# Softmax reciprocal as the exponential of a negative logarithm on ScalarE, and a third pairwise add on VectorE in the fourth block

## The chip, the cores and the metric

The kernel runs on one core of a Trainium2 chip. The metric is the device time of one execution in microseconds (us). The kernel before takes 184.47 us, the median of 4 runs that lie between 183.99 and 184.72. One further execution was recorded by the hardware profiler; all durations below are from that execution.

## The reference

The reference normalizes the input over its 512 features, and adds two branches to the input: a local attention with 32 heads of 16 features, and a gated feed-forward network.

```python
def _A_ref(x, wqkv, wo):
    B, S, D = x.shape              # 1, 2048, 512
    H = 32; Dh = D // H            # 16
    W, dil = 8, 2
    q, k, v = ...                  # x @ wqkv, split into 32 heads
    idx = pos[:, None] - off[None, :]      # off = 0, 2, ..., 14
    kg, vg = ...                   # keys and values at the 8 positions
    logits = jnp.einsum("bhsd,bhswd->bhsw", q, kg) * Dh ** -0.5
    logits = jnp.where(mask, logits, -1e9)
    attn = _softmax(logits, axis=-1)       # over 8 positions
    o = jnp.einsum("bhsw,bhswd->bhsd", attn, vg)
    return o.reshape(B, S, D) @ wo

def _B_ref(x, w_gate, w_up, w_down):       # 512 -> 1376 -> 512
    h = _gelu(x @ w_gate) * (x @ w_up)
    return h @ w_down

xn = _layernorm(x, axis=-1)
return x + _A_ref(xn, A_wqkv, A_wo) + _B_ref(xn, B_w_gate, B_w_up, B_w_down)
```

Each token attends to only eight positions, at distances 0, 2, ..., 14. So the logits are no matrix product over tokens; they are elementwise products of queries with shifted keys, summed over the 16 features of a head.

## The kernel before

**Blocks.** The 2048 tokens are cut into 4 blocks of 512. Feature data lies with features on the 128 partitions and the block's tokens along the free dimension, in four groups of 128 features. Each block passes through the same steps, and steps of neighbouring blocks are interleaved.

**Steps of block b**, with the names of the code. The input is normalized (`bnst`, `bnag`, `sub`, `norm`; on ScalarE also small steps `ve`, `vp`, `va`, `vb`) and transposed by DMA (`trx`, from block 1 on). TensorE computes the q, k and v projections (`mm<b>_<0,1,2>_<g>`, L1009, four matmuls each), and ScalarE copies them out of PSUM (`evq`, `evk`, `evv`, L1020). VectorE multiplies queries with the eight shifted keys (`pr<b>_<g>`, L1040, 128x4096), once for each of the four groups, and adds the products in pairs: `pa<b>_0` adds groups 0 and 1, `pa<b>_1` adds groups 2 and 3 (L1053). TensorE then sums over the features of a head with a matrix of constants, in `er<b>_3`. This task first computes a small part of the feed-forward network (L1078, 16 matmuls), and then, for each of the two half sums, 8 matmuls of 32x512 (L1085) that accumulate the logits in two PSUM banks.

**Softmax.** VectorE takes the maximum over the eight positions (`d1`, L1117) and subtracts it (`d2`, L1122). ScalarE takes the exponential (`exp`, L1131). VectorE adds the eight exponentials in three steps (`d4a`, `d4b`, `d4c`, L1138), takes the reciprocal of the 128x128 sums (`d5`, L1150) and multiplies (`d6`, L1155). Four DMAs write the result to a scratch tensor in DRAM (`ss`, L1164), and four read it back, spread over the features of each head, into PT (`sl`, L1176). VectorE multiplies it with the shifted values (`pv`, L1184), adds (`pw`, L1193, `pz`, L1199), and the attention's output stands in OT.

**Feed-forward and output.** TensorE computes the gate and up projections (`fg`, `fu`, L1217, four matmuls each, and `fg<b>_10`, L1256); ScalarE applies gelu (`gelu`, L1227, L1264) and copies the up half (`uev`, L1234, L1272); VectorE multiplies (`h`, L1241, L1279). The output tile of 128 tokens sums 4 matmuls with Wo and 11 with Wd (`acc...`, L1302). ScalarE copies it (`fe`, L1335), VectorE adds the input (`fin`, L1340, L1346), and a DMA stores it (`sto`).

**What sets the order.** The order of every engine's instructions is written out by hand in a table `ORDER`, one list of task names for each of TensorE ("pe"), ScalarE ("act"), VectorE ("dve"), GpSimd ("pool") and SyncE ("sp"), which issues all DMAs. An engine works through its list strictly in order; waits on other engines follow from the data and from the buffers. PSUM has eight banks, taken in the order in which tasks ask for them, so a TensorE task may also wait until another engine has read an older result out of a bank. `schedule` (L207) walks the lists to choose buffers and banks; `emit_engine` (L364) emits them. ScalarE holds one set of function tables at a time; where the next function is not in the set, the build puts a table load ahead of it. Identity and Square need no change of set here.

Of the kernel before, what the change touches and what calls it, by code (L numbers as in the profile page):

```python
# [135 lines left out]
class Graph:  # L136
# [252 lines left out]
    def report(self):  # L389
# [8 lines left out]
ACTF = mybir.ActivationFunctionType  # L398
# [6 lines left out]
    "pe":  # L405
        "warm0 warm1 warm2 warm3 warm4 warm5 warm6 warm7 warm8 warm9 tpx0_0 warm10 warm11 warm12 warm13 "
        "warm14 mma0_0 tpx0_1 mmt0_0 mmt0_1 mmt1_0 tpx1_0 mmt1_1 mmt0_2 tpx1_1 mmt1_2 mmt0_3 mmt1_3 "
        "mm0_2_0_0 mm0_2_3_0 mm0_2_2_0 mm0_2_1_0 fg0_0 fg0_1 fg0_2 fu0_0 fg0_3 fu0_1 fu0_2 fg0_4 fu0_3 fg0_5 "
        "fu0_4 fu0_5 fg0_6 fg0_7 er0_3 mm1_0_0_0 mm1_1_0_0 mm1_0_1_0 mm1_1_1_0 fg1_0 fu0_6 mm1_0_3_0 "
        "mm1_0_2_0 mm1_1_3_0 fu0_7 fu1_0 fg1_1 fg0_8 fu1_1 mm1_1_2_0 fu0_8 mm1_2_0_0 fg1_2 fg0_9 fu1_2 "  # L410
        "mm1_2_2_0 fg1_3 fu1_3 fu0_9 fg0_10 fg1_4 fu1_4 mm1_2_3_0 fg1_5 mm1_2_1_0 fg1_6 fu1_5 fu1_6 fg1_7 "
        "mm2_0_0_0 mm2_1_1_0 mm2_1_0_0 mm2_0_3_0 er1_3 mm2_0_1_0 fg1_10 mm2_1_2_0 mm2_2_1_0 mm2_0_2_0 fu1_7 "
        "fg2_0 accd1 mm2_1_3_0 accd2 fg2_1 mm2_2_3_0 mm2_2_2_0 fg1_8 fg2_2 acca0 fu2_0 accb0 fg1_9 mm2_2_0_0 "
        "accd3 er2_3 fu2_1 fu1_8 fu1_9 fu2_2 fg2_3 fu2_3 mm3_1_2_0 mm3_1_1_0 mm3_1_3_0 mm3_0_1_0 mm3_0_0_0 "
        "fg2_4 mm3_1_0_0 fu2_4 mm3_0_2_0 fg3_0 mm3_0_3_0 fu3_0 fg3_1 fg2_10 fg3_2 accd7 accd5 mm3_2_0_0 "
        "fg2_5 fu3_1 fg3_3 mm3_2_3_0 mm3_2_1_0 fu2_5 fu3_2 acca4 er3_3 accb4 fg3_4 accd6 fu3_3 fu3_4 fg2_6 "
        "fg3_5 fu2_6 fg2_7 fg3_6 fu2_7 fg2_8 fu2_8 fu3_5 fg3_7 fu3_6 mm3_2_2_0 fg2_9 fu3_7 fu2_9 fg3_8 fu3_8 "
        "fg3_9 fg3_10 acca8 accd10 accd9 fu3_9 accb8 accd11 acca12 accd13 accd14_0 accd14_1 accw14_0 "
        "accw14_1 accw13 accb12 accd15_0 accw12 accw15_0 accd15_1 accw15_1 accd15_2 accw15_2",
    "act":  # L420
        "c_tbl sx1 sq0 negm1 sxx1 sq1 evx0_0 evx0_1 evq0_0 sq2 evq0_1 evk0_0 evx1_0 sq3 evk0_1 bnst8 evx1_1 "
        "bnst9 evq0_2 sq6 evk0_2 evq0_3 evk0_3 ve8 evv0_0_0 sq4 vp8 bnag8 bnag9 va8 gelu0_0 evv0_2_0 "
        "evv0_3_0 bnst10 gelu0_1 bnst11 uev0_2 gelu0_3 vb8 gelu0_4 uev0_1 uev0_3 ve10 gelu0_5 uev0_4 uev0_0 "
        "uev0_5 gelu0_2 halo1 vp10 gelu0_7 bnag10 bnag11 evq1_0_0 evk1_0_0 evv0_1_0 evq1_1_0 evk1_1_0 "
        "gelu0_6 exp0 sub11 evq1_3_0 evk1_3_0 evq1_2_0 va10 uev0_7 uev1_0 uev0_10c uev0_6 sub9 vb10 sub8 "
        "uev1_1 evk1_2_0 norm9 uev0_10b gelu1_1 gelu1_0 norm8 gelu0_8 evv1_0_0 gelu1_2 sub10 uev0_8 bnst12 "
        "gelu0_9 norm11 uev1_2 uev0_9 norm10 evv1_2_0 gelu1_4 gelu1_3 uev1_3 evv1_1_0 uev1_4 uev1_5 uev0_10a "
        "bnst13 gelu1_5 gelu0_10 uev1_6 evk2_1_0 evv1_3_0 evk2_0_0 ve12 vp12 gelu1_7 bnag12 evq2_0_0 gelu1_6 "
        "evq2_1_0 uev1_10b bnag13 uev1_10c halv1 evk2_2_0 evq2_2_0 halo2 exp1 bnst14 sub12 bnst15 uev1_7 "
        "va12 ve14 vb12 uev1_10a vp14 bnag14 evk2_3_0 bnag15 evq2_3_0 evv2_1_0 va14 vb14 fe1 fe2 sub14 "  # L430
        "gelu2_0 evv2_2_0 halo3 gelu1_10 sub15 uev2_0 norm12 sub13 evv2_0_0 evv2_3_0 norm13 fe0 norm15 fe3 "
        "norm14 gelu1_8 gelu2_1 gelu1_9 uev2_1 uev1_8 uev2_2 uev1_9 uev2_3 gelu2_2 evk3_2_0 evk3_1_0 "
        "uev2_10b gelu2_3 exp2 evq3_1_0 evk3_3_0 evq3_2_0 evq3_0_0 halv2 evk3_0_0 uev2_10c evq3_3_0 uev2_4 "
        "uev2_10a gelu2_10 gelu3_1 uev3_0 gelu3_0 fe7 evv3_0_0 gelu2_5 gelu3_3 evv3_1_0 uev2_5 uev3_1 fe5 "
        "gelu2_4 gelu3_2 uev3_10c halv3 evv3_3_0 uev3_2 fe4 fe6 uev3_3 uev3_10b exp3 gelu3_5 uev2_6 gelu3_4 "
        "gelu2_7 uev2_7 uev2_8 gelu3_6 gelu2_6 evv3_2_0 gelu3_7 uev3_4 gelu2_8 gelu2_9 uev2_9 uev3_10a "
        "uev3_7 uev3_5 uev3_6 gelu3_10 fe10 gelu3_8 gelu3_9 uev3_9 fe9 uev3_8 fe8 fe11 fe13 fe12",
    "dve":
        "c_wdz bnst0 bnag0 sub0 rstd0 norm0 mean1 sub1 evy0_0 rstd1 norm1 evy0_1 bnst2 bnag2 sub2 rstd2 "
        "norm2 bnst3 bnag3 sub3 rstd3 norm3 bnst7 bnst6 bnst5 bnag6 bnag7 bnst4 bnag5 sub7 rstd6 bnag4 sub6 "  # L440
        "norm7 sub4 sub5 norm6 pr0_2 pr0_0 pr0_3 rstd4 pr0_1 norm4 norm5 pa0_1 pa0_0 h0_0 h0_1 h0_2 mask "
        "d1_0 d2_0 pr1_0 pr1_1 d4a_0 d4b_0 d4c_0 d5_0 rstd8 d6_0 pr1_3 pa1_0 pr1_2 h0_3 pa1_1 pv0_1 rstd10 "
        "pv0_3 h0_4 pv0_0 h1_1 pv0_2 pw0_1 h0_10 pw0_2 d1_1 pw0_3 d2_1 pz0 pr2_2 d4a_1 pr2_0 d4b_1 h1_3 "
        "d4c_1 h1_2 d5_1 h1_0 d6_1 pr2_1 pr2_3 pa2_0 fin1 rstd12 pa2_1 h1_10 pv1_1 rstd14 pv1_3 d1_2 pv1_0 "
        "d2_2 pv1_2 pw1_1 fin3 pw1_2 h2_1 pw1_3 h1_4 d4a_2 pz1 d4b_2 pr3_1 d4c_2 pr3_2 d5_2 fin0 d6_2 pr3_3 "
        "pr3_0 h2_0 h2_10 pa3_0 fin2 pa3_1 pv2_0 pv2_2 d1_3 pv2_1 d2_3 pw2_1 h3_1 d4a_3 h3_0 d4b_3 fin7 "
        "d4c_3 h2_2 d5_3 fin5 d6_3 pv2_3 pw2_2 h2_3 pw2_3 h2_4 pz2 fin4 pv3_3 pv3_0 pv3_1 fin6 pw3_1 fin10 "
        "h3_3 h3_10 pv3_2 h3_2 fin9 h3_4 pw3_2 fin8 pw3_3 fin11 pz3 fin14_0 fin14_1 fin13 fin15_0 fin15_1 "
        "fin12 fin15_2",
    "pool":  # L450
        "c_ones c_onef c_id c_vnpad c_idb c_eps c_mhalf c_e8a c_e8b c_e8c c_e8d c_ktpad c_mask0 c_mask1 "
        "c_utz sq8 sq10 sq12 sq14",
    "sp":
        "ld_x0_0 ld_x0_1 ld_wq ld_x1_0 ld_wk ld_x1_1 ld_wv ld_x2 ld_x4 ld_x3 ld_wg0 ld_wu0 ld_wt0 ld_x5 "
        "ld_wt1 trx3_0 ld_wt2 trx3_1 trx2_0 trx2_1 ld_wd0 ld_x6 ldxr1 ld_x7 ld_wd1 ld_wo ss0_2 ss0_3 ss0_0 "
        "ss0_1 ldxr2 sl0_1 sl0_3 sl0_2 trx4_0 sl0_0 trx4_1 trx5_1 trx5_0 ss1_2 ss1_3 ss1_1 ss1_0 sl1_1 sl1_3 "
        "sl1_0 sl1_2 ldxr3 trx6_0 trx6_1 trx7_1 trx7_0 sto3 sto1 ldxr0 ldxr7 ss2_1 ss2_2 ss2_3 ss2_0 sl2_0 "
        "sl2_3 sl2_2 sto0 sl2_1 sto2 ldxr5 ldxr4 sto5 ss3_0 ss3_1 ss3_2 ss3_3 ldxr10 sl3_3 sl3_0 sl3_2 sl3_1 "
        "ldxr6 sto4 sto6 ldxr8 ldxr9 sto9 ldxr11 ldxr14 sto8 sto7 sto10 ldxr13 sto11 sto14_0 sto14_1 ldxr15 "
        "ldxr12 sto13 sto15_0 sto15_1 sto12 sto15_2",  # L460
}
SCHED = dict(DMA_BPUS=290e3, DMA_FIXED=1.7)
# [6 lines left out]
def d_act(n):  # L469
    return 0.10 + 0.00085 * n  # L470
# [10 lines left out]
def bass_parallel_sum__sliding_local_dilated__glu_gated_geglu__prompt_kernel(nc, A_x, A_wqkv, A_wo, B_x, B_w_gate, B_w_up, B_w_down, out, dbg=None, cfg=None):  # L481
    cfg = dict(cfg or {})
# [26 lines left out]
    PACT = cfg.get("PACT", 4)  # L509
    PPOW = cfg.get("PPOW", 4)  # L510
    FIN2 = cfg.get("FIN2", tuple(range(14)))
    PR_ADD3 = cfg.get("PR_ADD3", ())
    WO_LAST = cfg.get("WO_LAST", (3,))
    CHAIN_SHIFT = cfg.get("CHAIN_SHIFT", [0, 300, 600, 900])
    FFN_BASE = cfg.get("FFN_BASE", 500)
# [8 lines left out]
    with contextlib.ExitStack() as es:  # L524
        block = es.enter_context(nc.Block())

        def sb(name, shape, dt):
# [14 lines left out]
        mask = sb("mask", [32, 2, 4, 16], F32)  # L542
# [7 lines left out]
        sums = sb("sums", [128, 3], F32)  # L550
# [6 lines left out]
        rc = sb("rc", [128, NMS, 128], FP16)  # L557
# [3 lines left out]
        EX = sb("EX", [128, 1024], FP16)  # L561
# [23 lines left out]
        G = Graph()  # L585
# [81 lines left out]
            rd=[I_mask], wr=[I_mask], prio=PC2 + 10)  # L667
# [275 lines left out]
        for b in range(NB):  # L943
# [156 lines left out]
            def lgv(p0, np_, dims, lg=it_lg):  # L1100
                return bass.AP(PS, p0 * 4096 + 512 * lg.slot, [[4096, np_]] + [[st, n] for (st, n) in dims])

            def msv(k, it=it_ms):
                return bass.AP(ms, (it.slot * 2 + k) * 128, [[NMS * 2 * 128, 128], [1, 128]])
# [23 lines left out]
            it_ex = Item("ex%d" % b, P_ex, "ex")  # L1128

            def mk_d3(lgv=lgv):  # L1130
                return lambda e: e.activation(out=EX[:, :], in_=lgv(0, 128, [(1, 1024)]), func=ACTF.Exp)  # L1131
            G.task("act", "exp%d" % b, d_act(1024), mk_d3(), rd=[it_lg], wr=[it_ex], prio=base + 32,
                   table="exp", batch=b)

            for k, w in enumerate((512, 256, 128)):
                def mk_d4(w=w, it=it_pb, msv=msv):
                    def f(e):
# [6 lines left out]
                       rd=[it_ex if w == 512 else I_su], wr=[(it_ms, 1) if w == 128 else I_su],  # L1144
                       prio=base + 33)

            def mk_d5(msv=msv, it=it_ms):
                def f(e):
                    with nc.allow_low_precision(reason="the reference holds the sums of exponentials in bf16"):
                        return e.reciprocal(out=rc[:, it.slot, :], in_=msv(1))  # L1150
# [266 lines left out]
```

## Time and profile before

| | |
|---|---|
| median of 4 runs | 184.47 us (183.99 to 184.72) |
| profiled execution: time / span | 184.45 us / 182.6 us |
| TensorE matmuls busy | 178.0 us, 98% of the span |
| VectorE busy | 169.7 us, 93% |
| ScalarE busy | 128.2 us, 70% |
| GpSimd busy | 9.5 us, 5% |
| mean rate of the DMAs | 107 GB/s |
| granted TensorE clock | 1.000 |

The span runs from the first to the last instruction of the core; the rest of the execution's time lies around it. In the profile's rows PE is TensorE's matmul stream, PEld its weight loads, DVE is VectorE, ACT is ScalarE, POOL is GpSimd and SP is SyncE; L and a number is a line of the kernel. A row of a group shows the line, the engine, the operation, what is written and read with its shape, the count, the busy time and the mean duration in ns, and after the second bar the idle time ahead of it. A row of the chain or of a timeline shows a start in us, a duration in us and what ran. Neighbouring instructions of one engine overlap a little, so the step from one start to the next is shorter than the duration.

### The profile page before, as it was taken

The page shows a single profiled execution, that of the slowest core. Times are in us where ns is not written, and L with a number is a line of the kernel's source. Part 1 is how long each engine was busy: PE and PEld are TensorE (multiplying, and loading weights), DVE is VectorE, ACT ScalarE, POOL GpSimd, SP SyncE. Part 2 cuts the span into 40 slices and gives each one's busy share as a digit, 9 for nine tenths or more (in the row PEclk, how much of TensorE's full clock was granted, in tenths as well). Part 3 has the DMA queues.
Part 4 walks back from the last instruction along what each step waited for, and adds up shares of the span by engine and source line. Part 5 has one row for each costly group of instructions (what it writes and reads, how often), then busy time and mean ns, then how long its engine had stood idle before and what let it go on. Part 6 is the DMA issues. An engine that isn't in the chain of part 4 may idle for free.

```text
span 182.6 us, 2790 instructions
## 1 busy us (share of the span) xinstructions
PE 178.0 (98%) x1068; PEld 90.1 (49%) x1068; DVE 169.7 (93%) x172; ACT 128.2 (70%) x258; POOL 9.5 (5%) x23
## 2 busy tenths in 40 slices
PE   8799999999999999999999999999999999999994
PEld 2796444544444544444444544444444444444664
DVE  3769999999999999999999999999999999999922
ACT  5688987999999899998695977527449764234011
POOL 6000010003200000122000000000000000000000
DMA  5999915932672000002851020128100355022433
GB/s 137 354 378 379 122 24 137 364 105 52 178 147 57 0 0 0 4 14 77 249 67 30 9 77 0 31 58 263 53 0 0 92 149 196 0 86 61 140 103 102
DMA packets 26220, 19.60 MB, mean 107 GB/s; under 512 B 13824, under 2 KB 23008, under 8 KB 26208
## 3 DMA queue, kind: packets, MB, share of 16 engines
q1 hardware_dynamic: 26208, 19.44, 37.9%
q8 instruction: 8, 0.13, 0.3%
q14 instruction: 4, 0.03, 0.1%
HBM read 14.71 MB, written 3.15 MB: 98 GB/s over the span
## 4 chain that ended last, share of the span: by engine, by line
PE 94%; DMA 2%; ACT 1%; SPq 0%; issue 0%; DVE 0%; DVEq 0%
PE PS L1217 38%; PE PS L1302 29%; PE PS L1009 19%; PE PS L959 4%; DMA Wqkv<-in_A_wqkv_dram 2%; PE PS L1085 2%; PE PS L1256 2%; PE PS L1078 1%; SPq L731 0%; ACT KT L986 0%; ACT xnT L919 0%; PE PS L899 0%; DVE OB L1346 0%; DVEq L376 0%
## 5 line engine op out<-in xcount | busy, mean ns | idle before, releaser
L1302 PE MATMUL PS<-Wd,HT 128*128 128x512 bf16 (+2 forms) x209 | 41.0, 345 | 0.0
L1217 PE MATMUL PS<-xnT,Wg 128*128 128x512 bf16 x160 | 39.8, 379 | 0.0
L1217 PE MATMUL PS<-xnT,Wu 128*128 128x512 bf16 x160 | 39.1, 379 | 0.0
L1009 PE MATMUL PS<-xnT,Wqkv 128*128 128x512 bf16 x160 | 38.0, 379 | 0.0
L1184 DVE TENSOR_TENSOR UNI<-VN,PT 128x4096 f16<-128x4096 bf16 x16 | 36.3, 2282 | 0.0
L1040 DVE TENSOR_TENSOR UNI<-QT,KT 128x4096 f16<-128x4096 bf16 x16 | 36.1, 2283 | 0.0
L1302 PEld LDWEIGHTS PS<-Wd,HT 128*128 128x128 bf16 x209 | 19.6, 98 | 19.2 <-issue 0.4
L1234 ACT ACTIVATE UU<-PS 128x512 bf16<-128x512 f32 x40 | 23.1, 600 | 6.4 <-PE PS L1217 6.1
L1193 DVE TENSOR_TENSOR UNI<-UNI 128x4096 f16<-128x4096 f16 x12 | 27.4, 2285 | 0.0
L1227 ACT ACTIVATE GG<-PS 128x512 bf16<-128x512 f32 x40 | 22.9, 602 | 5.8 <-DVE HT L1241 5.8
L1009 PEld LDWEIGHTS PS<-xnT,Wqkv 128*128 128x128 bf16 x160 | 17.9, 113 | 16.9 <-issue 0.8
L1217 PEld LDWEIGHTS PS<-xnT,Wu 128*128 128x128 bf16 x160 | 15.6, 98 | 19.0 <-ACT XIN L853 0.4
L1217 PEld LDWEIGHTS PS<-xnT,Wg 128*128 128x128 bf16 x160 | 15.7, 98 | 18.7
L1335 ACT ACTIVATE OB<-PS 128x512 bf16<-128x512 f32 x14 | 8.3, 601 | 17.3 <-PE PS L1302 15.1
L1053 DVE TENSOR_TENSOR UNI<-UNI 128x4096 f16<-128x4096 f16 x8 | 18.2, 2282 | 0.0
L1302 PE MATMUL PS<-Wo,OT 128*128 128x512 bf16 (+2 forms) x76 | 16.5, 345 | 0.0
L1020 ACT ACTIVATE VN<-PS 128x512 bf16<-128x512 f32 x16 | 9.3, 596 | 6.5 <-PE PS L1009 6.5
L1241 DVE TENSOR_TENSOR HT<-GG,UU 128x1024 bf16<-128x1024 bf16 x20 | 13.5, 682 | 0.0
L832 POOL TENSOR_TENSOR sq<-ve,mhalf 128x2 bf16<-128x2 f32 x4 | 6.6, 1658 | 72.7 <-ACT ve L828 72.7
L1302 PEld LDWEIGHTS PS<-Wo,OT 128*128 128x128 bf16 x76 | 7.1, 98 | 6.6 <-issue 0.3
L1272 ACT ACTIVATE UT<-PS 64x256 bf16<-64x256 f32 (+1 forms) x12 | 5.4, 447 | 6.7 <-PE PS L1256 3.9
L959 PE MATMUL PS<-xnT,Wqkv 128*128 128x128 bf16 x128 | 8.1, 219 | 0.8 <-DMA Wqkv<-in_A_wqkv_dram 0.7
(85 smaller groups left out, 158.1 us busy)
## 6 DMA issues: line engine op xcount, KB each, us to landing
PT<-pt_scratch SPq DMA_DIRECT2D x16, 256.0 KB, 4.2
XR<-in_A_x_dram SPq DMA_DIRECT2D x16, 128.0 KB, 2.2
out_dram<-OB SPq DMA_DIRECT2D x14, 128.0 KB, 2.0
Wqkv<-in_A_wqkv_dram SPq DMA_DIRECT2D x3, 512.0 KB, 5.3
XIN<-in_A_x_dram SPq DMA_DIRECT2D x6, 256.0 KB, 6.4
Wg<-in_B_w_gate_dram SPq DMA_DIRECT2D x1, 1280.0 KB, 8.4
Wu<-in_B_w_up_dram SPq DMA_DIRECT2D x1, 1280.0 KB, 11.3
Wd<-in_B_w_down_dram SPq DMA_DIRECT2D x1, 1280.0 KB, 6.3
```

What stands on the lines that cost most here:

```text
L959: ins = e.matmul(PS[:, 512 * it.slot + 128 * g:512 * it.slot + 128 * g + 128], lhsT=wcols(which, kt, g), rhs=xnT[:, itx.slot, kt, t * 128: ...
L1009: ins = e.matmul(PS[:, 512 * it.slot:512 * it.slot + 512], lhsT=wcols(which, kt, g), rhs=xnT[:, itx.slot, kt, :], start=(kt == 0), stop=(k ...
L1020: return e.activation(out=o, in_=PS[:, 512 * it.slot:512 * it.slot + 512], func=ACTF.Identity, scale=(QSC, 1.0, 1.0)[which])
L1040: return lambda e: e.tensor_tensor(out=UNI[:, it.slot, :, :], in0=bass.AP(QT, (itq.slot * 4 + g) * 512, [[NQT * 4 * 512, 128], [0, 8], [1, ...
L1053: return lambda e: e.tensor_tensor(out=UNI[:, i0.slot, :, :], in0=UNI[:, i0.slot, :, :], in1=UNI[:, i1.slot, :, :], op=ALU.add)
L1184: return lambda e: e.tensor_tensor(out=bass.AP(UNI, ito.slot * 4096, [[NUNI * 4096, 128], [2048, 2], [512, 4], [1, 512]]), in0=bass.AP(VN, ...
L1193: return lambda e: e.tensor_tensor(out=UNI[:, i0.slot, :, :], in0=UNI[:, i0.slot, :, :], in1=UNI[:, i1.slot, :, :], op=ALU.add)
L1217: ins = e.matmul(PS[0:M, 512 * it.slot:512 * it.slot + 512], lhsT=Wx[:, kt, j * 128:j * 128 + M], rhs=xnT[:, itx.slot, kt, :], start=(kt = ...
L1227: return lambda e: e.activation(out=GG[:, ito.slot, q, :], in_=PS[:, 512 * it.slot:512 * it.slot + 512], func=ACTF.Gelu_apprx_tanh)
L1234: return lambda e: e.activation(out=UU[:, ito.slot, q, :], in_=PS[:, 512 * it.slot:512 * it.slot + 512], func=ACTF.Identity)
L1241: return lambda e: e.tensor_tensor(out=HT[:, ito.slot, j - 1:j + 1, :], in0=GG[:, ig.slot, :, :], in1=UU[:, iu.slot, :, :], op=ALU.mult)
L1302: ins = e.matmul(PS[:, 512 * it.slot:512 * it.slot + CW], lhsT=(OT[:, ito.slot, q, ti * 128:(ti + 1) * 128] if kind == "o" else HT[:, ith. ...
```

## The change

It has three parts.

First, the reciprocal of the softmax sums leaves VectorE. ScalarE computes the logarithm of the sums in place (`ln`), and then the exponential of the negative logarithm (`d5`, now a ScalarE task). The exponential of the logits names the table set that holds both functions.

Second, in block 3 (`PR_ADD3`) VectorE adds the two half sums (`pa3_2`), and `er3_3` reads this one sum, with 8 matmuls at L1085 in place of 16.

Third, the lists of `ORDER` are new for all engines but GpSimd. The places that matter below are shown; each list has been reordered in most of its rows.

```diff
     "pe":
...
-        "mm0_2_0_0 mm0_2_3_0 mm0_2_2_0 mm0_2_1_0 fg0_0 fg0_1 fg0_2 fu0_0 fg0_3 fu0_1 fu0_2 fg0_4 fu0_3 fg0_5 "
-        "fu0_4 fu0_5 fg0_6 fg0_7 er0_3 mm1_0_0_0 mm1_1_0_0 mm1_0_1_0 mm1_1_1_0 fg1_0 fu0_6 mm1_0_3_0 "
...
-        "fg2_4 mm3_1_0_0 fu2_4 mm3_0_2_0 fg3_0 mm3_0_3_0 fu3_0 fg3_1 fg2_10 fg3_2 accd7 accd5 mm3_2_0_0 "
...
+        "mm0_2_2_0 mm0_2_1_0 fg0_0 mm0_2_0_0 fg0_1 fg0_2 fg0_3 fu0_0 fu0_1 mm0_2_3_0 fg0_4 fu0_2 fu0_3 fu0_4 "
+        "fg0_5 mm1_1_0_0 mm1_0_0_0 fu0_5 fg0_6 er0_3 mm1_0_1_0 mm1_1_1_0 fg0_7 mm1_1_3_0 mm1_0_2_0 mm1_2_3_0 "
+        "fg1_0 mm1_0_3_0 mm1_1_2_0 fg1_1 fu1_0 fu1_1 fu0_6 fu0_7 fg1_2 fu1_2 mm1_2_2_0 mm1_2_1_0 fg1_3 fu1_3 "
...
+        "fu1_7 accd1 mm2_2_2_0 fu1_8 acca0 fg1_10 mm2_2_3_0 accb0 fg2_1 fg2_2 accd3 fg2_3 fu2_0 fg1_9 fu2_1 "
+        "mm2_2_1_0 fu2_2 fu2_3 er2_3 mm3_1_0_0 mm3_1_3_0 fu1_9 mm3_0_0_0 mm3_1_2_0 mm3_0_2_0 mm3_2_1_0 "
+        "mm3_0_1_0 mm3_1_1_0 fg3_0 mm3_0_3_0 fg2_4 mm3_2_0_0 mm3_2_2_0 mm3_2_3_0 fu3_0 fu2_4 fg2_5 fg2_10 "
+        "accd7 fu2_5 fg3_1 fu3_1 fg3_2 accd5 acca4 er3_3 fg2_6 accb4 accd6 fu2_6 fg2_7 fg2_8 fg3_10 fu2_7 "
...
     "act":
...
+        "exp0 sub8 va10 evq1_2_0 vb10 ln0 sub11 d5_0 evk1_3_0 evq1_3_0 evv1_3_0 uev1_0 evk1_2_0 sub9 uev1_1 "
...
+        "uev1_4 evq2_3_0 gelu1_7 bnag13 evq2_1_0 halo2 evk2_3_0 exp1 bnst14 va12 bnst15 vb12 ve14 evk2_2_0 "
+        "vp14 uev1_10b bnag14 ln1 uev1_7 d5_1 sub13 halv1 fe2 bnag15 uev1_8 va14 vb14 sub15 sub12 fe1 "
+        "uev1_10c evv2_2_0 sub14 norm12 norm13 fe0 evv2_3_0 evv2_0_0 gelu2_2 gelu2_1 norm14 fe3 norm15 halo3 "
+        "gelu1_9 evq3_0_0 evk3_0_0 evq3_2_0 evk3_3_0 evk3_2_0 evq3_1_0 exp2 halv2 evk3_1_0 uev1_9 evv3_0_0 "
+        "evv3_3_0 ln2 evv3_2_0 evq3_3_0 d5_2 evv3_1_0 uev3_0 halv3 gelu2_5 uev2_10a gelu2_4 uev2_5 uev2_4 "
+        "uev3_1 fe5 gelu2_10 gelu3_1 fe7 fe4 uev3_10c gelu3_2 gelu3_0 exp3 uev3_10b uev2_6 uev2_7 fe6 ln3 "
+        "uev3_2 d5_3 uev2_8 gelu2_6 uev3_3 gelu2_7 gelu2_9 uev2_9 gelu2_8 gelu3_4 gelu3_5 uev3_5 gelu3_3 "
...
     "dve":
...
-        "d1_0 d2_0 pr1_0 pr1_1 d4a_0 d4b_0 d4c_0 d5_0 rstd8 d6_0 pr1_3 pa1_0 pr1_2 h0_3 pa1_1 pv0_1 rstd10 "
...
+        "sub7 pr0_1 rstd6 rstd4 norm7 norm5 norm6 pr0_0 norm4 pr0_3 pr0_2 pa0_0 pa0_1 pr1_0 mask d1_0 h0_1 "
+        "d2_0 pr1_1 h0_2 d4a_0 d4b_0 d4c_0 pa1_0 d6_0 pr1_3 pr1_2 h0_3 rstd8 pa1_1 h0_0 h1_0 rstd10 pv0_1 "
...
+        "pr2_2 d6_1 pr2_3 pa2_0 rstd12 pa2_1 h1_3 fin2 h1_2 pv1_0 rstd14 pv1_2 pv1_3 pv1_1 h1_10 pw1_1 d1_2 "
+        "h2_1 pa3_2 pv2_1 d1_3 h2_10 d2_3 fin3 pv2_0 h2_2 d4a_3 pv2_2 d4b_3 h3_0 d4c_3 pw2_1 d6_3 pw2_2 fin7 "
...
     FIN2 = cfg.get("FIN2", tuple(range(14)))
-    PR_ADD3 = cfg.get("PR_ADD3", ())
+    PR_ADD3 = cfg.get("PR_ADD3", (3,))
     WO_LAST = cfg.get("WO_LAST", (3,))
...
             it_ex = Item("ex%d" % b, P_ex, "ex")
 
             def mk_d3(lgv=lgv):
-                return lambda e: e.activation(out=EX[:, :], in_=lgv(0, 128, [(1, 1024)]), func=ACTF.Exp)
-            G.task("act", "exp%d" % b, d_act(1024), mk_d3(), rd=[it_lg], wr=[it_ex], prio=base + 32,
-                   table="exp", batch=b)
+                def f(e):
+                    e.preload_act_table_set("natural_log_exp_and_others")
+                    return e.activation(out=EX[:, :], in_=lgv(0, 128, [(1, 1024)]), func=ACTF.Exp)
+                return f
+            t_ex = G.task("act", "exp%d" % b, d_act(1024), mk_d3(), rd=[it_lg], wr=[it_ex], prio=base + 32,
+                          table="exp")
 
             for k, w in enumerate((512, 256, 128)):
                 def mk_d4(w=w, it=it_pb, msv=msv):
...
                        rd=[it_ex if w == 512 else I_su], wr=[(it_ms, 1) if w == 128 else I_su],
                        prio=base + 33)
 
+            def mk_ln(msv=msv):
+                return lambda e: e.activation(out=msv(1), in_=msv(1), func=ACTF.Ln)
+            G.task("act", "ln%d" % b, 0.21, mk_ln(), rd=[(it_ms, 1)], wr=[(it_ms, 1)], prio=base + 34, table="exp")
+
             def mk_d5(msv=msv, it=it_ms):
-                def f(e):
-                    with nc.allow_low_precision(reason="the reference holds the sums of exponentials in bf16"):
-                        return e.reciprocal(out=rc[:, it.slot, :], in_=msv(1))
-                return f
-            G.task("dve", "d5_%d" % b, 0.87, mk_d5(), rd=[(it_ms, 1)], wr=[(it_ms, 2)], prio=base + 34)
+                return lambda e: e.activation(out=rc[:, it.slot, :], in_=msv(1), func=ACTF.Exp, scale=-1.0)
+            G.task("act", "d5_%d" % b, 0.21, mk_d5(), rd=[(it_ms, 1)], wr=[(it_ms, 2)], prio=base + 34, table="exp")
 
             def mk_d6(it=it_ms, ito=it_pb):
                 return lambda e: e.tensor_tensor(
```

## The prediction

> **What bounds the kernel now.** I read the page first (busy time, chain), then the chain piece by piece, then the timelines of VectorE and ScalarE at the places the change touches, then the groups by line. Page and chain:
>
> ```profile
> span 182.6 us, 2790 instructions
> PE 178.0 (98%) x1068; PEld 90.1 (49%) x1068; DVE 169.7 (93%) x172; ACT 128.2 (70%) x258; POOL 9.5 (5%) x23
> PE 94%; DMA 2%; ACT 1%; SPq 0%; issue 0%; DVE 0%; DVEq 0%
> ```
>
> TensorE carries 94% of the chain that ends last. "Busy" is not proof of a full stream, so the pieces in order of time matter more:
>
> ```profile
> 14.71 3.45 PE PS L1009 x16
> 18.16 12.09 PE PS L1217 x56
> 30.25 0.21 issue
> 30.47 0.62 PE PS L1078 x16
> 31.09 0.86 PE PS L1085 x16
> ...
> 64.88 0.55 PE PS L1078 x16
> 65.43 0.86 PE PS L1085 x16
> ...
> 129.02 0.55 PE PS L1078 x16
> 129.57 0.86 PE PS L1085 x16
> ```
>
> 3.45 us for 16 matmuls of 512 columns is 0.216 us each, and from 14.71 to the end the pieces join at this pitch. The one idle piece is 0.21 us at 30.25, before `er0_3`; the first part of `er0_3` also takes 0.62 us instead of 0.55. So only two things shorten this kernel: fewer matmul columns, or removing about 0.28 us (0.21 + 0.07) at `er0_3`. All other engines work under TensorE's cover, and can only lengthen it, by making TensorE wait.
>
> What is missing at 30.25 shows on VectorE:
>
> ```profile
> 25.88 4.49 DVE L1053 TENSOR_TENSOR UNI<-UNI 128x4096 f16<-128x4096 f16 x2
> 30.28 1.89 DVE L1241 TENSOR_TENSOR HT<-GG,UU 128x1024 bf16<-128x1024 bf16 x3
> ```
>
> The second pairwise add of block 0 ends at 25.88 + 4.49 = 30.37, and `er0_3` starts 0.10 later.
>
> **The change, part by part.**
>
> *Fewer columns in `er3_3`.* In block 3 the two half sums are added on VectorE (`pa3_2`), so L1085 runs 8 matmuls instead of 16. Sixteen take 0.86 us, because four column strips run together; eight take 0.43. **Saved on the path: 0.43 us.** The eight weight loads that go lie beside matmuls and save nothing more.
>
> *`er0_3` moves.* The new order puts 19 groups of four matmuls ahead of it in this stage instead of 18 (two of block 1's q/k projections come forward, one `fu` group goes back). The stage's first matmul starts at 14.55, so TensorE arrives at 14.55 + 19 × 4 × 0.216 = 30.97 instead of 30.11. VectorE has the same instructions ahead of the two adds as before, so they still end by about 30.4, 0.5 us early. **Saved: 0.28 us.** The projections brought forward (`mm1_1_0_0`, at 27.5) need block 1's transposes: the move of `norm4` ahead of two products lets the last of the four issue at about 22.0 instead of 27.6; with 3.2 us to landing (median 3.1) it is there at 25.2, 2.3 us early. Nothing else is late there.
>
> *The third add.* One more addition of 128x4096:
>
> ```profile
> L1053 DVE TENSOR_TENSOR UNI<-UNI 128x4096 f16<-128x4096 f16 x8 | 18.2, 2282 | 0.0
> L1150 DVE RECIPROCAL rc<-ms 128x128 f16<-128x128 f32 x4 | 3.8, 947 | 0.0
> L1131 ACT ACT_TABLE_LOAD x4 | 5.1, 1283 | 0.1
> L1131 ACT ACTIVATE EX<-PS 128x1024 f16<-128x1024 f32 x4 | 4.1, 1023 | 0.0
> L1028 ACT ACTIVATE KT<-KT 128x64 bf16<-128x64 bf16 x3 | 0.8, 261 | 0.0
> ```
>
> It lasts 2.28 us; as neighbours overlap by 0.08, it moves VectorE's queue by 2.20. The four reciprocals moved it by 0.87 each (0.95 less overlap), 3.48 together. Net VectorE is relieved by 1.28 us, worth nothing directly since TensorE covers it. The dangerous moment is `er3_3`: up to it three reciprocals are gone (-2.61) and one add has come (+2.20). Following VectorE's new order with these row durations, `pa3_2` ends at 126.85; TensorE, counting matmuls, arrives at 127.48. Spare: 0.63 us. Without this cover the delay would pass to TensorE one for one, up to 2.2.
>
> *Logarithm and second exponential on ScalarE.* No row is a 128x128 activation. From 64 elements (0.261) to 1024 (1.023) is 0.79 ns an element, so about 0.31 us each: I take 0.30, with 0.26 and the 512-element 0.60 as ends. Eight take 2.4 us, 1.6 of queue time after the overlap of 0.1. ScalarE is idle for 30% of the span, but it works in order, and `ln` waits for VectorE's last small sum. Block by block: `ln0` waits some 0.2 us; `ln1` about 1.0 (it reaches the head at 75.6, the sum ends at 76.6); `ln2` and `ln3` find their sums ready. Behind `ln1` stand `uev1_7`, `d5_1`, `sub13` and then `fe2`, `fe1` and `fe0`, which free PSUM banks that TensorE wants at `mm2_2_3_0` and `accd3`; but before `fe1` ScalarE waits another 1.5 us for `fu1_8` anyway. That swallows the delay of `ln1`, and `fe1` ends 0.7 us before TensorE needs its bank. In the other direction VectorE fills the detour with a 128x4096 product or addition placed between the small sum and `d6` in every block: `d5` ends 0.9 to 2.4 us before `d6` comes up, so `d6` doesn't wait. At 0.60 us each the eight would cost TensorE 0.1 to 0.2 (at `fu1_1` and `fg2_9`); this goes into the range.
>
> *The table set.* In the built program loads stand at the exponential and at the next gelu, none at `ln` or `d5`: ten in both kernels. The load of the common set hasn't run here. The row says 1.28 us, and the timeline no pause around it:
>
> ```profile
> 136.59 0.38 ACT L1272 ACTIVATE UT<-PS 64x256 bf16<-64x256 f32 x1
> 136.98 1.28 ACT L1131 ACT_TABLE_LOAD   x1
> 138.28 1.02 ACT L1131 ACTIVATE EX<-PS 128x1024 f16<-128x1024 f32 x1
> ```
>
> The Trainium skill, page "ScalarE: Activation LUTs", section "What ACT_TABLE_LOAD costs", speaks against the change here: it adds a drain of about 1.38 us to every switch to another set, 2.66 in all, while holding the load itself to be equal for every set. The sharpest place for it is block 2. From the start of `mm3_0_1_0` to that of `mm3_2_0_0`, which needs the bank that `exp2` empties, lie five groups: 5 × 0.864 = 4.32 us. ScalarE's detour: matmul group 0.86, its last result 0.16, signal 0.06, `evq3_1_0` 0.48, load 1.30, `exp2` 1.02 = 3.88. By the row 0.44 us are left, cost 0; by the page's 2.66 TensorE waits 0.92, and the net gain of 0.71 becomes a loss of 0.2. I take the row: in this trace 1.30 separate the end before the load from the exponential.
>
> *Queues of SyncE.* The same 100 transfers are reordered. `d6` to the first landing of the table in PT took 7.9, 7.9, 7.9 and 7.4 us in the four blocks. With `d6` ending at 42.4, 79.4, 116.5 and 141.1 in the new order the first one lands 0.6, 0.2, 2.2 and 2.1 us before VectorE comes to `pv`. Block 1 is tight, but VectorE then has about 0.3 us of waiting and 0.63 at `er3_3` to give. No transfer moves into the tail.
>
> *The tail.* Last products, output adds and stores stand in nearly the same order; `pz3` ends 0.5 us before `accw14_0` (before: 173.09 to 173.57, also 0.5). Unchanged.
>
> **Sum.** -0.43 - 0.28 = -0.71 us. The profiled execution took 184.45 (span 182.6 and 1.85 around it), so 183.74; it lies 0.02 under the median of 184.47. From the median: **183.75 us**, -0.39%.
>
> **The rivals.** I call 0.3% (0.55 us) what a measurement of this kernel can tell from no change: the limits are 183.92 and 185.02.
>
> *A, the sum holds:* 183.75 (183.4 to 183.92). For it: every TensorE wait I followed in the new order keeps 0.44 us or more. Chance 0.68.
>
> *B, partly eaten:* the order has some ten places with only 0.44 to 0.6 us spare (`er0_3`, `er1_3`, `accd2`, `er2_3`, `mm3_2_0_0`, `fu3_6`, `accw14_0` among them); one or two slips of 0.3 give back the 0.28, or `er0_3` waits for a bank instead of VectorE. 183.74 + 0.3 = 184.05, up to 184.7. Against it: the old order had 0.10 to 0.3 spare at `er0_3` and `accd1` and 0.16 at `fu2_4`, and lost only at the first. Chance 0.19.
>
> *C, slower: the switch to the common set is longer than the old one.* With x us more, `mm3_2_0_0` waits x - 0.44; in block 0 `exp0` ends at 38.3 and `mm1_1_2_0` comes for its bank at 39.3, so it waits x - 1.0. At the full 1.38 that is 0.94 + 0.38 = 1.32, and 183.75 + 1.32 = 185.07; with what follows later in ScalarE's queue up to 186. It becomes a loss from x of about 1.1, where the two waits exceed the 0.71. Against it: equal 1283 ns in all groups of loads here. Chance 0.10.
>
> *D, it doesn't do what it says:* a reload at each `ln` and `d5` would add two switches a block, 8 × 1.3 = 10.4 us on ScalarE, over 187. The built program excludes the loads, unless the hardware part differs. Chance 0.03.
>
> **How the numbers follow.** A is the likeliest, so 183.75. Faster is A: 0.68; same is B with the mild end of C: 0.20; slower the rest of C and D: 0.12. The range leaves out D and most of C: 183.3 (A less the scatter of the runs, 183.99 to 184.72) to 184.6 (most of B).
>
> **What would show it.** L1085's 56 matmuls, with 0.43 us after the last L1078 piece; no "issue" before the first; no new TensorE wait; a load row still x4 at 1283 at the exponential, none at the logarithm; the two small activations near 0.30; PE busy near 177.5 and a span near 181.9. A piece of ACT, DVE or idle in the chain between 14.7 and 180 would make the prediction wrong, above all before `mm3_2_0_0` or `er3_3`.

## The result and the profile after

The changed kernel takes 184.07 us (median of 35 runs, 183.59 to 184.5) against 184.38 for the kernel before (56 runs, the four of the section above among them). The ratio is 0.9984, 95% interval 0.9978 to 0.999: 0.16% faster, about 0.3 us. That is a real gain, but less than half of the forecast 0.71 us, and inside what I had called no change (0.3%). It lies in the range 183.3 to 184.6. Of the four cases rival B, "partly eaten", came true.

The page of the changed kernel first: span, busy time, chain.

```profile
span 182.1 us, 2777 instructions
PE 178.0 (98%) x1060; PEld 89.9 (49%) x1060; DVE 168.7 (93%) x169; ACT 129.3 (71%) x266; POOL 11.1 (6%) x23
PE 90%; DMA 8%; SPq 1%; issue 0%; DVE 0%; DVEq 0%
```

TensorE still sets the end, VectorE is relieved by 1.0 us and ScalarE has 1.1 more. New is the DMA share of the chain: 8% in place of 2%. The chain in order of time (start, duration, what) names the transfer:

```profile
8.07 8.36 DMA Wg<-in_B_w_gate_dram
16.43 0.05 issue
16.47 1.04 PE PS L1221 x4
...
29.60 1.73 PE PS L1221 x8
31.32 0.55 PE PS L1078 x16
31.88 0.86 PE PS L1085 x16
...
128.08 0.55 PE PS L1078 x16
128.63 0.43 PE PS L1085 x8
```

The steps of the forecast can be read here. The piece "issue" ahead of the first L1078 is gone, and this piece takes 0.55 us like the others, so `er0_3` no longer waits. In block 3, L1085 takes 0.43 us for 8 matmuls. No run undoes the change at `er0_3` alone; what it is worth follows below from the stretch that all traces share. But the chain now runs through the load of the gate weights, which lands at 16.43; the first gate matmul starts right after it. TensorE's timeline at this place:

```profile
14.53 1.89 PE L1009 MATMUL PS<-xnT,Wqkv 128*128 128x512 bf16 x8
16.47 1.04 PE L1221 MATMUL PS<-xnT,Wg 128*128 128x512 bf16 x4
```

Eight matmuls from 14.53 at 0.216 us end their turn at 16.26, so TensorE stands still for 0.21 us. The new order has `fg0_0` as the third group of its stage, the old one had it as the fifth. Rows of the kernel before: the issue of the load on SyncE, its size and time to landing, and TensorE's timeline.

```profile
8.08 0.37 SPq L696 DMA_DIRECT2D Wg<-in_B_w_gate_dram  x1
Wg<-in_B_w_gate_dram SPq DMA_DIRECT2D x1, 1280.0 KB, 8.4
18.00 2.75 PE L1217 MATMUL PS<-xnT,Wg 128*128 128x512 bf16 x12
```

So the load itself hasn't changed: issued at 8.08, it was there at 16.48, 1.5 us before TensorE used it at 18.00.

The last output add starts 0.50 us earlier than before (last piece of the chain, first before, then after):

```profile
180.18 0.29 DVE OB L1346
179.68 0.29 DVE OB L1350
```

That is 0.43 + 0.28 - 0.21 = 0.50. So in this one execution the balance is closed. The medians show 0.31; whether the missing 0.2 has the same cause is what the experiments ask first.

### The profile page after: what moved, and what is told of

Read it like the earlier page. It is cut to its first block, busy times and chain, and to the rows that moved or that the text cites. A ratio compares the mean times of both kernels' runs of the same rounds, so it can differ in the third digit from the quotient of the medians.

```text
span 182.1 us, 2777 instructions
## 1 busy us (share of the span) xinstructions
PE 178.0 (98%) x1060; PEld 89.9 (49%) x1060; DVE 168.7 (93%) x169; ACT 129.3 (71%) x266; POOL 11.1 (6%) x23
## 4 chain that ended last, share of the span: by engine, by line
PE 90%; DMA 8%; SPq 1%; issue 0%; DVE 0%; DVEq 0%
PE PS L1221 38%; PE PS L1306 29%; PE PS L1009 18%; DMA Wg<-in_B_w_gate_dram 5%; DMA Wqkv<-in_A_wqkv_dram 3%; PE PS L1260 2%; PE PS L1085 2%; PE PS L1078 1%; SPq L731 1%; SPq L687 0%; DVE OB L1350 0%; DVEq L376 0%
## 5 line engine op out<-in xcount | busy, mean ns | idle before, releaser
L1009 PE MATMUL PS<-xnT,Wqkv 128*128 128x512 bf16 x160 | 37.9, 379 | 0.0
L1197 DVE TENSOR_TENSOR UNI<-UNI 128x4096 f16<-128x4096 f16 x12 | 27.4, 2282 | 0.0
L1009 PEld LDWEIGHTS PS<-xnT,Wqkv 128*128 128x128 bf16 x160 | 17.9, 114 | 16.9 <-ACT UU L1238 0.4
L1053 DVE TENSOR_TENSOR UNI<-UNI 128x4096 f16<-128x4096 f16 x9 | 20.4, 2281 | 0.0
L832 POOL TENSOR_TENSOR sq<-ve,mhalf 128x2 bf16<-128x2 f32 x4 | 8.2, 2058 | 72.6 <-ACT ve L828 72.6
L1020 ACT ACTIVATE QT<-PS 128x512 bf16<-128x512 f32 x12 | 7.2, 597 | 3.2 <-PE PS L1009 3.2
L959 PE MATMUL PS<-xnT,Wqkv 128*128 128x128 bf16 x128 | 8.2, 219 | 0.7 <-DVE XIN L873 0.6
```

The source lines that it names most:

```text
L832: "pool", "sq%d" % t, 7.0, lambda e, t=t, n=n: e.tensor_tensor(out=sq[:, t:t + n], in0=ve[:, t:t + n], in1=mhalf[:, 0:n], op=ALU.pow),
L1009: ins = e.matmul(PS[:, 512 * it.slot:512 * it.slot + 512], lhsT=wcols(which, kt, g), rhs=xnT[:, itx.slot, kt, :], start=(kt == 0), stop=(k ...
L1020: return e.activation(out=o, in_=PS[:, 512 * it.slot:512 * it.slot + 512], func=ACTF.Identity, scale=(QSC, 1.0, 1.0)[which])
L1053: return lambda e: e.tensor_tensor(out=UNI[:, i0.slot, :, :], in0=UNI[:, i0.slot, :, :], in1=UNI[:, i1.slot, :, :], op=ALU.add)
L1197: return lambda e: e.tensor_tensor(out=UNI[:, i0.slot, :, :], in0=UNI[:, i0.slot, :, :], in1=UNI[:, i1.slot, :, :], op=ALU.add)
```

## The experiments

Theory: the forecast's sum holds for everything behind `fg0_0`, and the loss is the wait for the gate weights alone. Rivals: the loss lies in small waits spread over the order; the third add pays by itself and the moved reciprocal is idle decoration; ScalarE's waits cost what VectorE gains.

To compare traces I use one stretch: from the start of the last small q/k matmul (L959) to the start of the last output add. It leaves out the start-up, which scatters. In some traces a few matmul records are missing, so that a gap of 0.2 us without a cause in them is no wait (one with `fg0_0` fifth has 1044 of 1060, and the same stretch as the other one, which has all); the ends of the stretch are not touched by this.

### The changed kernel again

> The changed kernel once more, as the neighbour of the other runs. The trace of the changed kernel ends its last output add 0.50 us earlier than the trace before (180.18 to 179.68): 0.43 fewer columns and 0.28 at er0_3, less a new wait of 0.21 for the gate weights before fg0_0. Theory (the forecast's sum less that new wait): 0.3 to 0.5 us under the kernel before, and a TensorE gap of about 0.2 us before fg0_0 at 16.3. Rival (the first profile was a lucky one): no gap there, and the gain differs by more than 0.2 us from 0.31.

184.07 us, the kernel before beside it 184.37; ratio 0.9993 (0.9975 to 1.001), an interval that includes no change at all. The profiled execution contradicts the theory's second half: it has no wait before `fg0_0`, as the rival had said. Its small q/k matmuls end later (the last starts at 14.83 in place of 14.48), TensorE comes for `fg0_0` at 16.61, and the weights had landed at 16.35. Its stretch is 164.97 us, against 165.20 in the first profile and 165.69 before. So without the wait the gain behind the start-up is 0.72 us, and the forecast said 0.71. Whether the wait occurs depends on how early the execution starts, and on when the weights land.

### `fg0_0` one group later

```diff
-"mm0_2_2_0 mm0_2_1_0 fg0_0 mm0_2_0_0 fg0_1 ...
+"mm0_2_2_0 mm0_2_1_0 mm0_2_0_0 fg0_0 fg0_1 ...
```

> The changed kernel with fg0_0 behind mm0_2_0_0, one group of four later, all else equal. Theory (the missing part of the forecast went into the wait for the gate weights, which land at 16.43 while TensorE is at fg0_0 at 16.26): TensorE comes at 17.12, the wait is gone, the time falls by 0.2 us against the changed kernel, to about 0.7 us under the kernel before. If the weights usually land later than in the profile, it falls by up to 0.5. Rival (the missing part lies elsewhere, in waits that only other executions have): under 0.1 us of difference to the changed kernel.

183.75 us, ratio to the kernel before 0.9973 (0.9963 to 0.9982): 0.62 us under it and 0.32 under the changed kernel beside it. The wait is gone, and the stretch is 164.97. In this execution the weights landed only at 17.35, TensorE came at 17.64; one group of delay was just enough.

### Without the third add

```diff
-    PR_ADD3 = cfg.get("PR_ADD3", (3,))
+    PR_ADD3 = cfg.get("PR_ADD3", ())
-... fin0 h2_1 pa3_2 pv2_1 ...
+... fin0 h2_1 pv2_1 ...
```

> The changed kernel without the third pairwise add: pa3_2 is taken out of VectorE's list and er3_3 has its 16 matmuls at L1085 again. Theory: TensorE has 0.43 us more on its path and nothing else changes, so 0.43 us above the changed kernel, about 0.1 us above the kernel before. Rival (VectorE's 2.2 us for the add already delay what comes behind it): less than 0.25 us above the changed kernel, or below it.

184.58 us, 0.51 above the changed kernel and 0.21 above the kernel before (ratio to the latter 1.0009, 0.9995 to 1.0022). The chain shows the 16 matmuls again:

```profile
127.96 0.55 PE PS L1078 x16
128.51 0.86 PE PS L1085 x16
```

The stretch is 165.71: 164.97, plus 0.43 for the columns, plus 0.29 of wait for the gate weights (TensorE at `fg0_0` at 16.06, landing at 16.30 and 0.05 more). The 0.43 is shown, and VectorE's 2.2 us for the add cost nothing in this order.

### The third add alone

This edit is made to the kernel before, all others to the changed kernel.

```diff
-    PR_ADD3 = cfg.get("PR_ADD3", ())
+    PR_ADD3 = cfg.get("PR_ADD3", (3,))
-... fin2 pa3_1 pv2_0 ...
+... fin2 pa3_1 pa3_2 pv2_0 ...
```

> The kernel before with the third pairwise add alone, pa3_2 right behind pa3_1, and er3_3 with 8 matmuls; the reciprocal stays on VectorE. Theory (the add needs the time that the reciprocals leave, and spare at er3_3): pa3_1 ended at 127.64, pa3_2 ends 2.2 later at 129.84, TensorE comes for er3_3 at 128.95, so it waits about 1 us; later places behind exp3 and the h products wait up to another 1.2 us; less 0.43. So 0.5 to 1.7 us above the kernel before. Rival (the add pays by itself): 0.4 us below the kernel before.

186.87 us, ratio 1.014 (1.012 to 1.0159): 2.5 us slower, above the expected 0.5 to 1.7. TensorE's waits of this kernel (who waited for whom, total, times, longest):

```profile
PE PS L1078 <- DVE UNI L1053: 1.0, 1, 1.0
PE PS L1302 <- DVE OT L1199: 0.8, 1, 0.8
```

The first is `er3_3` behind the add, as worked out. The second wasn't expected by name: `pz2` comes late, and with it the output tile `acca8`. VectorE, once behind by 2.2 us, carries the delay on. The stretch is 167.49, 1.80 above that of the kernel before. Behind it, the last store of the output takes 2.6 us from issue to landing, against 1.6 in the kernel before, and 1.8 + 1.0 is more than the 2.5 of the medians. Why this store is slower, and whether it was so in the three executions without a trace, stays open. The same add costs 2.5 us in the old order, with the reciprocals on VectorE, and gains about half a microsecond in the new order without them. The orders differ too, so this pair alone doesn't show that the reciprocals make the difference; the run with the reciprocal back on VectorE, below, keeps the new order.

### `fg0_0` fifth, and `fg0_0` second

```diff
-"mm0_2_2_0 mm0_2_1_0 fg0_0 mm0_2_0_0 fg0_1 fg0_2 fg0_3 fu0_0 fu0_1 mm0_2_3_0 fg0_4 ...
+"mm0_2_2_0 mm0_2_1_0 mm0_2_0_0 mm0_2_3_0 fg0_0 fg0_1 fg0_2 fg0_3 fu0_0 fu0_1 fg0_4 ...
```

> The changed kernel with both mm0_2_0_0 and mm0_2_3_0 ahead of fg0_0, so that fg0_0 is the fifth group as in the kernel before. Theory (the only loss against the forecast is the wait for the gate weights, whose landing scatters between 16.2 and 17.4 from execution to execution, while the fourth group starts at about 17.1): the time is that of the run with one group of delay, 183.75, or up to 0.1 us less where the weights come late; 0.6 to 0.75 us under the kernel before. Rival (something else holds back the rest): no better than 184.0.

184.08 us against 184.47 before; ratio 0.9977 (0.9961 to 0.9992). The stretch is 164.97 again, but the median missed the expectation and is what the rival said (no better than 184.0). This comparison ran on another chip than the one with the fourth place, and was repeated below.

```diff
-"mm0_2_2_0 mm0_2_1_0 fg0_0 mm0_2_0_0 ...
+"mm0_2_2_0 fg0_0 mm0_2_1_0 mm0_2_0_0 ...
```

> The changed kernel with fg0_0 one group earlier, behind mm0_2_2_0 alone. TensorE comes for it at 15.4 and the gate weights land at 16.4, so it waits 1.0 us in place of 0.2. Theory (nothing behind can catch up, since TensorE's stream is full): 0.85 us above the changed kernel, 184.9. Rival (the wait is absorbed later): less than 0.4 us above the changed kernel.

184.7 us, ratio to the kernel before 1.002 (1.0007 to 1.0034), so 0.5 to 0.6 us above the changed kernel (whose ratio was 0.9984 to 0.9993), rather than 0.85, and above the rival's limit of 0.4. TensorE's timeline:

```profile
14.36 1.03 PE L1009 MATMUL PS<-xnT,Wqkv 128*128 128x512 bf16 x4
16.68 1.04 PE L1221 MATMUL PS<-xnT,Wg 128*128 128x512 bf16 x4 [1.30 <-DMA Wg<-in_B_w_gate_dram]
```

TensorE's turn came at 14.36 + 0.86 = 15.22, the matmul starts at 16.68: 1.46 us of wait (the row counts idle time from the last matmul's modelled end, 1.30). The stretch grows to 166.45 = 164.97 + 1.48. Nothing behind it catches up. That the median rises by less than one group's 0.86 would follow if executions that don't wait at `fg0_0` in the changed kernel first use up what they have to spare there.

### Third, fourth and fifth place side by side

> The changed kernel, the kernel with fg0_0 fourth and the one with fg0_0 fifth, now beside each other on one chip. In the traces so far the stretch from the last small q/k matmul to the last output add is 164.97 us where TensorE doesn't wait for the gate weights, and 165.20 in the first profile, where it waited 0.21. Theory: the changed kernel loses this wait only in executions whose TensorE is early at fg0_0; its median is 0.2 to 0.4 us above the other two and 0.3 under the kernel before. Rival (the differences so far came from the chips): the three agree within 0.1 us.

> As said for the run beside it: 0.5 to 0.7 us under the kernel before, 0.2 to 0.4 under the changed kernel; the trace has no gap before fg0_0 and 164.97 us from the last small q/k matmul to the last output add. Rival: no different from the changed kernel.

> As said for the two runs beside it: the same as with fg0_0 fourth, within 0.1 us. If it is 0.2 us or more slower than that one, the fifth place costs something that the stretch to the last output add doesn't show.

| kernel | median us | ratio to before (184.34) | stretch |
|---|---|---|---|
| changed (third) | 184.19 | 0.9991 (0.9981 to 1.0001) | 164.97 |
| `fg0_0` fourth | 183.64 | 0.9963 (0.9951 to 0.9974) | 164.97 |
| `fg0_0` fifth | 183.72 | 0.9963 (0.995 to 0.9976) | 164.97 |

On one chip the fourth and the fifth place agree within 0.1 us, both are 0.5 us better than the third, and 0.6 to 0.7 under the kernel before. The intervals of third and fourth don't touch. The rival is refuted, and so is the fear that the fifth place costs something. The gain of the fourth place, 0.70 us, is close to the forecast's 0.71 (0.62 in the first comparison). The changed kernel itself did worse than expected: 0.15 us under the kernel before in place of 0.3, and about 0.5 above the other two in place of 0.2 to 0.4. TensorE's timeline with the fourth place:

```profile
14.65 2.54 PE L1009 MATMUL PS<-xnT,Wqkv 128*128 128x512 bf16 x11
17.03 2.32 PE L1221 MATMUL PS<-xnT,Wg 128*128 128x512 bf16 x10
```

14.65 + 11 × 0.216 = 17.03, so nothing lies between (one of the twelve records is missing).

All traces of these orders together, with the time at which TensorE's turn for `fg0_0` comes, the landing of the gate weights, and the wait:

| trace | turn | landing | wait | stretch |
|---|---|---|---|---|
| before (fifth) | 18.00 | 16.48 | 0 | 165.69 |
| changed, first profile | 16.26 | 16.43 | 0.21 | 165.20 |
| changed, again | 16.61 | 16.35 | 0 | 164.97 |
| changed, third time | 16.80 | 16.70 | 0 | 164.97 |
| no third add | 16.06 | 16.30 | 0.29 | 165.71 |
| fourth, two traces | 17.64, 17.03 | 17.35, 16.16 | 0 | 164.97 |
| fifth, two traces | 18.84, 17.80 | 16.33, 16.49 | 0 | 164.97 |
| second | 15.22 | 16.64 | 1.46 | 166.45 |

Each stretch of the new orders is 164.97 plus the wait, plus 0.43 where the add is missing, within 0.02. For the kernel before, 165.69 - 164.97 - 0.43 leaves 0.29: the stall at `er0_3`, forecast as 0.28. An execution that starts early gives its lead back at `fg0_0` in the changed kernel; the kernel before kept it.

The waits of executions without a trace can't be seen. The medians on the same chip differ by 0.32 and 0.55 us (184.07 and 184.19 less 183.75 and 183.64). The traces explain only a part of this: the three of the changed kernel waited 0.21, 0 and 0. As an estimate, start-up and landing of each of the thirteen traces of all kernels here (the landing and 0.05, less the turn, 8 × 0.216 behind the first large matmul) give what the third place would have waited: 0 to 0.6 us, 0.19 on average, and nothing in the fourth place. So the edit shows that the third place costs 0.3 to 0.55 us, and the traces show a wait there, but they don't show all of it; the rest stays open.

### The reciprocal back on VectorE

The edit is shown for one block and made in all four.

```diff
 dve: -... d4c_0 pa1_0 d6_0 ...
      +... d4c_0 d5_0 pa1_0 d6_0 ...
 act: -... vb10 ln0 sub11 d5_0 evk1_3_0 ...
      +... vb10 sub11 evk1_3_0 ...
```

> The changed kernel with the reciprocal back on VectorE, right behind the last small sum of each block; logarithm and second exponential are gone from ScalarE, all other places stay. Theory (the move's worth is the VectorE time in front of er3_3): up to pa3_2 three reciprocals put 2.6 us more on VectorE, the spare at er3_3 is 0.70, so TensorE waits about 1.9 us in all at er3_3 and at places that VectorE holds back before it (accd2, the h products), and up to 1 us more at fu3_6 behind h2_3: 2 to 3 us above the changed kernel. Rival (VectorE has time enough and ScalarE's waits at ln cost as much): within 0.5 us of the changed kernel.

188.13 us (four runs, 187.17 to 189.21), ratio 1.0195 (1.0157 to 1.0232): 3.7 us above the kernel before beside it (184.47), and 4.1 above the changed kernel, which ran on another chip. TensorE's waits:

```profile
PE PS L899 <- DVE mv L763: 0.8, 1, 0.8
PE PS L1220 <- ACT GG L1230: 0.8, 1, 0.8
PE PS L1009 <- ACT UU L1237: 0.7, 1, 0.7
PE PS L1078 <- DVE UNI L1053: 0.5, 1, 0.5
```

The stretch is 167.88, 2.9 above 164.97, inside the expected 2 to 3. The wait at `er3_3` (L1078) is only 0.5; TensorE has lost 0.7 before it, at L1009. The two rows with ACT come through ScalarE, which waits for products that VectorE delivers late; the one at L1220 is `fu3_6`, as foreseen. The first row lies in the start-up, where this kernel has the same instructions as the changed one, and this execution was the slowest of the four. Here, too, the last store takes 2.6 us to land in place of 1.6, which the theory had not; with it 3.9 us of this execution are accounted for. Not run: the new order with the reciprocals on VectorE and without the add. So it isn't shown how much of the loss falls on the add alone.

### Without naming the common table set

```diff
-                    e.preload_act_table_set("natural_log_exp_and_others")
```

> The changed kernel without the naming of the common table set, so that table loads stand at ln and at d5 as well, 18 in all. Theory (loads cost 1.3 us of ScalarE each; two more in a block make ln and d5 late by 2.6): ScalarE's spare at the banks is 0.6 to 1 us, so TensorE waits about 2 us in block 0 (fu1_1), 1 us in block 1 (behind fe2), 0.5 at er3_3, and 2 to 3 us in block 3: 5 to 6.5 us above the changed kernel. Rival (a switch costs 2.66 us each with its drain): 12 us or more above it. Rival (ScalarE's idle 30% hides them): under 1 us above it.

190.5 us, ratio 1.0309 (1.0273 to 1.0344): 6.0 us above the kernel before beside it, and 6.4 above the changed kernel of the other chip, in the expected 5 to 6.5. ScalarE's timeline in block 0 (exponential, logarithm, second exponential):

```profile
36.12 1.28 ACT L1132 ACT_TABLE_LOAD   x1
37.42 1.02 ACT L1132 ACTIVATE EX<-PS 128x1024 f16<-128x1024 f32 x1
...
39.52 0.29 ACT L828 ACTIVATE ve<-vb,eps 128x2 f32<-128x2 bf16 x1
39.83 1.28 ACT L1150 ACT_TABLE_LOAD   x1
41.13 0.31 ACT L1150 ACTIVATE ms<-ms 128x128 f32<-128x128 f32 x1
41.34 0.71 ACT L846 ACTIVATE XIN<-XIN,nmean 128x512 bf16<-128x512 bf16 x1
42.07 1.28 ACT L1154 ACT_TABLE_LOAD   x1
43.36 0.31 ACT L1154 ACTIVATE rc<-ms 128x128 f16<-128x128 f32 x1
```

Each load costs 1.28 us and starts 0.02 after the instruction ahead of it has ended (39.52 + 0.29 = 39.81). The first place to break is the one foreseen, with the largest of TensorE's waits:

```profile
PE PS L1220 <- ACT KT L1020: 1.9, 1, 1.9
PE PS L1220 <- ACT UU L1237: 1.1, 1, 1.1
PE PS L1220 <- ACT GG L1230: 0.9, 1, 0.9
```

The second and third rows are in block 3, and `er3_3` waits 0.3; the wait foreseen in block 1 did not come.

There is one more cost, which the theory didn't have. TensorE's timeline behind the longest wait (the first row of the list above), and its granted clock from 45.08 to 48.49 (stretch, its length, TensorE busy, clock, share and rate of the DMAs):

```profile
44.21 4.45 PE L1220 MATMUL PS<-xnT,Wu 128*128 128x512 bf16 x12 [1.95 <-ACT KT L1020]
48.50 1.03 PE L1220 MATMUL PS<-xnT,Wg 128*128 128x512 bf16 x4
45.08:48.49 3.41, 3.41 (x9) 0.50 0.32 77
```

From 44.21 to 48.50 twelve matmuls take 4.29 us where 12 × 0.216 is 2.59. The granted clock was 0.50 for most of this time, and that cost 1.7 us. Two more executions have a mean granted clock of 0.991, and with this one they take 190.48 to 190.86 us; the fourth has 1.000 and takes 189.18. So, by this one execution, the loads at full clock cost about 5 us, the low end of the forecast, and it is partly luck that the median of 6.4 lies inside it. The rival's 2.66 us for a switch is the figure that the prediction cites and doubts; here a switch takes 1.30, and 6.4 is far from the rival's 12.

Two more switches in a block turn a gain into a loss of 3%, although ScalarE is idle for 29% of the changed kernel's span.

## Why the prediction was half right

**Fewer columns in `er3_3`: right.** 0.43 us in the chain, and 0.5 us in the median when it is undone.

**`er0_3` moves: right in its size, wrong in "nothing else is late there".** This is the step that failed. TensorE arrived at `er0_3` late enough, and lost nothing there. I asked what the groups brought forward need, and checked block 1's transposes (they were in time). I didn't ask the same of `fg0_0`, which the new order brings from the fifth to the third place. With numbers of the profile before, turn 14.55 + 8 × 0.216 = 16.28 against a landing at 8.08 + 8.4 = 16.48, the wait of 0.2 could have been written down. The stall of 0.28 at `er0_3` was removed, and a stall of 0.21 came at `fg0_0` in the first trace; the medians put the loss at 0.32 and 0.55. A slip without weight: the group that goes behind `er0_3` is `fg0_7`, not one of the `fu` groups; the count of 19 holds. The rival named the pattern (`er0_3` waits for something else), but not this place.

**The third add: right.** The forecast had `pa3_2` end at 126.85 with 0.63 us to spare; VectorE's timeline has

```profile
119.68 4.48 DVE L1053 TENSOR_TENSOR UNI<-UNI 128x4096 f16<-128x4096 f16 x2
...
125.02 2.28 DVE L1053 TENSOR_TENSOR UNI<-UNI 128x4096 f16<-128x4096 f16 x1
```

so it ends at 127.30, and `er3_3` starts at 128.01: 0.71. Both ends lie about half a microsecond later than forecast, so the spare is the forecast's while the times are not. That the move of the reciprocals gives the cover fits both sides: the add without the move costs 2.5 us in the old order, and taking the move back costs about 3 us in the stretch. VectorE's busy time fell by 1.0 us where the forecast had 1.28, without consequence.

**Logarithm and second exponential: right.** Groups by line:

```profile
L1132 ACT ACT_TABLE_LOAD x4 | 5.1, 1283 | 0.1
L1151 ACT ACTIVATE ms<-ms 128x128 f32<-128x128 f32 x4 | 1.2, 308 | 0.8 <-DVE ms L1141 0.7
L1155 ACT ACTIVATE rc<-ms 128x128 f16<-128x128 f32 x4 | 1.2, 308 | 0.0
```

0.308 us each against 0.30. ScalarE waits 0.7 us for a small sum, once, at `ln1`, where I had 1.0; and it then waits for `fu1_8`, as said, so nothing of it reaches TensorE.

**The table set: right to take the row.** The load of the common set takes 1283 ns like all others. At the sharpest place ScalarE's timeline reads

```profile
105.89 0.60 ACT L1020 ACTIVATE QT<-PS 128x512 bf16<-128x512 f32 x1 [0.15 <-PE PS L1009]
106.50 1.28 ACT L1132 ACT_TABLE_LOAD   x1
107.79 1.02 ACT L1133 ACTIVATE EX<-PS 128x1024 f16<-128x1024 f32 x1
```

`exp2` ends at 108.81 and `mm3_2_0_0` starts at 109.14, without a wait. The 2.66 us that the Trainium skill ("ScalarE: Activation LUTs", "What ACT_TABLE_LOAD costs") gives for a switch would have pushed `exp2` past this start by 1 us; in this trace the switch takes 1.30, and the measurement decides. Rival C falls with it. Rival D was real in its mechanism: without the name the loads come, and cost about 5 us at the full clock, 6.4 in the median, rather than "over 3".

**SyncE's queues and the tail: nothing seen to the contrary.** VectorE comes to `pv` without a wait in all four blocks, and the last stores follow as before.

**The chances.** With each landing checked, 183.75 would have been the forecast for `fg0_0` in fourth place (183.64 and 183.75 measured), and about 183.95 for this kernel (183.75 and a wait of 0.2). I gave 0.68 to A because I had followed ScalarE and VectorE through the new order, and had taken the early loads as given.

## What to carry to other kernels

When a stream is full, every group that a new order moves forward has to be checked against everything it reads, the weights included: the time of its turn (a count of instructions times a pitch) against the landing that the page lists. In these traces a wait early in the full stream was not recovered (1.46 us of wait, 1.48 in the stretch), and it acts as a floor: executions that start early lose their lead there. A change that moves work between engines is worth what it lets another edit do; here the moved reciprocal earns nothing by itself on the path (without the add, 184.58 us against 184.37 before), but gives VectorE the time for the add that shortens it. When an experiment opens a gap in TensorE's stream, the granted clock behind the gap has to be read too, before the whole loss is put down to the gap.

## What I had not expected of the hardware

The start-up scatters more than the effect under study: the last small q/k matmul started between 14.27 and 15.33 us in twelve traces of these kernels with equal start-up lists (16.21 in the run with the reciprocal back on VectorE), and the gate weights landed between 15.59 and 17.35. Behind it, and without a wait for these weights, TensorE's stretch repeats to 0.02 us. So a wait that shows in one profile and not in the next can be the same cause, met earlier or later.

The halved clock came behind the longest gap in TensorE's stream behind the start-up in all thirteen traces, 1.95 us, began 0.9 us after the gap and lasted 3.4 us; behind the next longest, 1.30 us at `fg0_0` in second place, the clock stayed at 1.0. Where between the two the limit lies, and whether the length alone decides, no run here shows.

The version with `fg0_0` in fourth place beats both kernels: 0.9963 of the time of the kernel before, interval 0.9951 to 0.9974.
